# Fused attention and two expert layers: unsplit fp32 scores for two more head pairs, small additions on ScalarE, GpSimd differences in pieces

## The chip, the cores and the metric

The kernel runs on one core of a Trainium2 chip. The metric is the device time of one execution in microseconds (us). The engines are called by the names of the profile: PE (TensorE), DVE (VectorE), ACT (ScalarE), POOL (GpSimd) and SP (SyncE, which issues most of the DMAs). PEld is the load of weights into PE.

## What is computed

Thresholded attention over 4 batches, 8 heads, 576 positions and 64 dimensions per head, then a dense layer with a nonlinearity, then a layer of 8 experts of which each token takes one. All inputs and outputs are fp32.

```python
scores = q @ k.T / sqrt(64)                      # per batch and head
thresh = scores.max(-1) - tau
scores = where(scores >= thresh, scores, -1e9)
attn = exp(scores - scores.max(-1))
attn = attn / (attn.sum(-1) + 1e-9)
x = attn @ v                                     # tokens 2304, width 512
h = x @ w_in                                     # 512 -> 2048
x = (h - tanh(h)) @ w_out                        # 2048 -> 512
# per token: the expert e of the largest of x @ w_gate
y = gate * sigmoid((x @ w_output_gate)[e]) * (relu(x @ w1[e]) @ w2[e])
```

## The kernel before

The work is one long list of operations, written down by a planner in the file itself (class `Sched`): each call `sc.add(engine, duration, due, fn, reads, writes)` adds one operation, and the order in which the operations are emitted on each engine comes from a packed table of numbers, `URGENCY`, one number for each operation. Every engine then works through its own list in that order; an operation whose inputs are not there holds up all behind it on its engine.

Attention goes by units: batch, half of the positions, head pair (4 x 2 x 4 = 32 units, `units`). Batches are counted from 0 in the code, so the second batch is `b == 1`. A unit of the first half has 4 score tiles, one of the second half 5 (the fifth, called merged, holds the last 64 positions of both heads), 144 tiles in all. For each tile (function `attention`):

- PE computes the scores into the PSUM tile `sp`. In the first batch (`full`, the constant `FULL`) this is done in plain fp32, with 64 of the array's rows for one half of the columns and 64 for the other (line 1096). In the others, q and k have been split into two parts of fewer bits, so that four faster matmuls give the same (line 1085).
- DVE reads `sp` from PSUM, writes the negated scaled scores `em` and their minimum `mx` (line 1106). ACT takes the exponential, `e` (line 1109). A threshold `tb = mx + tau` is made on DVE for the two heads of a tile pair at once (line 1118). DVE masks `e` by it and sums (line 1122).
- PE transposes (line 1138), ACT copies the result to `eth`, PE multiplies with V (`pv`, line 1193, in two bursts of 3 and 2 key blocks), and the result is scaled by the reciprocals: on DVE an addition of 1e-9 to the sums `rs` of the unit (line 1160), a reciprocal (line 1162), on ACT and POOL the spread matrices `rb`; the product with them is `xf` (line 1212).

The split of q and k is made by ACT (rounded part, `round_to`) and POOL (difference, `rest`), in `prep_q` and `prep_k`. `rest` cuts POOL's difference into two halves where it has more than `HALVE` = 400 columns. The same helper makes POOL's differences for the dense layer's weights (`wi`, `wo`, from `conv`, whose five steps for a block run on ACT and DVE), for its activations (`gl`) and for the attention's output (`xl`). All DVE and POOL instructions of this kind read and write SBUF; line 1106 reads PSUM.

The dense layer (function `step`, lines 743 and 777, tiles `ph` and `x`) is interleaved with the attention as soon as the first 256 tokens are complete, and fills PE's time between the attention's matmuls. Its weights are stored and fetched again. The expert layer follows after all tokens (lines 1637, 1750, 1783). Buffers are rings: `em` has 5, `e` 3 (`EN`), `rb` 3 (`RBN`).

Of the kernel before, what the change touches and what calls it, by code (L numbers as in the profile page):

```python
# [17 lines left out]
ALU = mybir.AluOpType  # L18
# [3 lines left out]
P = 128  # L22
# [6 lines left out]
CH = 256  # L29
# [20 lines left out]
HALVE = 400  # L50
FULL = 8
EARLY = 4
EMN, EN, ETN, RBN = 5, 3, 2, 3
# [28 lines left out]
    'c-rk)_e0I^`+n_p_Bm}WqbRdfA{k{gsFV_gG^vo35s{EmR%GN|WF{+ARyJj&ge0<8Ml!NWzW4L$^Iv>De#m*9bDrlO*L_{rb24W{Y~J<E^zPq+'  # L82
    '8H0`2J<ACSua*BeJtTN*M&IV|;fvEYmpGpG+ZFq6U4%dD7VBweWWrVdSa2~~mzrN`=UzQII^M2R1@Y-vX*fNp$#=(@@Mz}2y{huJ9Q|~uO>c9%'
    '+hxvAjz>4G^j=Ch&F);+ZMk9bTccMaVssXDy}#@IwLJ<y{nC)w;;JI)I1_xLPM6@C#doi4J>zFEYv<kdm1Z%WUfeWpmSheH(chdEW%)L&xWG5L'
    'aBpidJ=hKp?5s`;vY7w-N8ql9GqsBk4VYP^iCJ*<q21U%^Hy{Y-sC*wlB?dgMTx$KEi0}rk5rUnQ++mmKC>g%XJ@V%u@Ad^ys)#@%hSY?5aN-w'
    'jeb?e?ebgB>b<=riQWDVi5jqaoaq*qSy`d8H@q3@UezsJ?`n#txm874QOTQ~kE&MvB+K|ihEIFZ-v>V!QR<r~_kLUU?PS&CXKY!6{p?Z83H>2g'
    'k{g$q&j~s8ZnFC7@$z!((}^pO+YO)9G{LtZB;mo8HBYb1xKbN<xZf&y{$t0`;x<1s8|-#jxsThH<)4^ZrFQ1{O+%Y&`UeL%>37K1RCqk^IIo9E'
    't$){hkC*3|o=8+MIWmvr$%-|1J688Muz2d>KHVnxSc0la?*#q9Y&G8Me=_n|Xv(&=Khl&FhXfuNGoa-*6Gd!OccunMyKPF}-0%7eZ~K--p$D`r'
    '^Uep<$sYM$IOTunkZp6!@w6WN*B!Q(p3m0G5kl(y3YHGv;PiN5*zCT+JL>`h2iIM#KAVy^dETIP)w1PP>w^vqsb8(Hs`^=+f5Fu8?(YRQWo6p8'
    '7w-7oafa2>ng12M%CG2TX07_F7&zVB>g8S4%NTXRCc`P6PE4Ek^H={9(@VaXnyzT*dM)9)bI$TbQ;Q1&_f*vSzbYf=pQt}PARuAJ0ea#~yY2HW'  # L90
    '>bFNEoHH-o>bJ6M>dWIUznW@3F3`O0Ww}N6GiSh%Wt;XFYHDw#H+FdO+V4ul=BSmf7UA};y<8gl1s?X^RI<56NBT)`>`U4GCSg|Mp~M1>*N!c!'
    'Qhr-#B7QbRGU=Ah!T96}zm<L2micdOHa}hbcjKZt_yzB#_kj^n|7D-{p3$@WSK@1ZxP_C?rDZucmF4@*^?wQ3^^z<n*Xp<<YU8L2t%GA7PsBz|'
    '5?bbr^M4YXPfyZhGX7Bmlhz#es<4Rea<P8$%T33WdJ$TadtHcJdAt)LX&p#k@6h*RpBFltHk^BL^=IYrVe5=PY&p2{o3mA$$?Ec*POtkjSvl*a'
# [318 lines left out]
def pool_tt(n):  # L412
    return int(2.11 * n + (145 if n > 400 else 110 if n < 256 else 60))
# [1564 lines left out]
```

## Time and profile before

| | |
|---|---|
| time, median of 3 runs | 970.16 us (969.92 to 971.55) |
| the profiled execution | 971.04 us |
| its span on the core | 969.2 us |
| PE busy | 940.4 us (97%), 6636 matmuls |
| DVE busy | 727.5 us (75%) |
| ACT busy | 551.1 us (57%) |
| POOL busy | 346.0 us (36%) |

The profiled execution took 971.04 us from end to end, of which 969.2 us are the span from the first to the last instruction. Busy time is the union of an engine's instructions. A PE that is busy is not always at its peak, since matmuls overlap. PE's clock was granted in full through nearly the whole span (1.00 in every stage up to 953 us). Where an engine was idle, the profile names what ended the wait. The score tiles of the first batch run from 4.6 to 83.5 us, and the last score tile at 454.7 us.

### The profile page before, as it was taken

The numbers are of one execution on the slowest core, as the hardware profiler recorded it, in microseconds if no ns is written. First come the engines' busy times: TensorE is split into PE (matmuls) and PEld (weight loads), VectorE is DVE, ScalarE is ACT, GpSimd is POOL, SyncE is SP. The second block draws the span as 40 slices with busy tenths as digits, with TensorE's granted clock in tenths as the row PEclk, the third lists the DMA queues.
The fourth block names the chain that finished last, engine by engine and source line by source line (L and its number), as shares of the span: only waits on it lengthen the run. The fifth ranks groups of instructions, "written<-read, shape, count | busy, mean of one in ns | idle before, by whom it ended". The sixth has DMA issues, their size and how long they took to land.

```text
span 969.2 us, 18499 instructions
## 1 busy us (share of the span) xinstructions
PE 940.4 (97%) x6636; PEld 806.5 (83%) x6636; DVE 727.5 (75%) x1812; ACT 551.1 (57%) x1142; POOL 346.0 (36%) x434
## 2 busy tenths in 40 slices
PE   8899889999999999999999999999999999999996
PEld 4556667888888888888899888888888899999996
DVE  7999999898789877857268668888676777646630
ACT  5888777777778767757445444344343434435421
POOL 1368548884667754434210101011012302213101
PEclk9999999999999999999999999999999999999999
DMA  9264645565664662451595366476854876655600
GB/s 268 102 204 150 195 139 183 170 206 169 198 215 160 193 244 86 132 182 45 180 364 175 118 189 158 130 169 137 266 177 144 271 229 229 193 169 165 214 14 32
DMA packets 71604, 168.70 MB, mean 174 GB/s; under 512 B 32382, under 2 KB 33022, under 8 KB 65616
## 3 DMA queue, kind: packets, MB, share of 16 engines
q1 hardware_dynamic: 67872, 157.41, 51.3%
q0 software_dynamic: 3200, 9.77, 2.9%
q8 instruction: 54, 0.88, 0.4%
q14 instruction: 46, 0.38, 0.1%
q10 hardware_dynamic: 432, 0.26, 0.1%
HBM read 125.99 MB, written 35.45 MB: 167 GB/s over the span
## 4 chain that ended last, share of the span: by engine, by line
PE 81%; DVE 14%; issue 2%; ACT 1%; DMA 1%; POOL 0%; POOLq 0%; DVEq 0%; ACTq 0%
PE x L777 20%; PE ph L743 20%; PE ph L1750 9%; PE py L1637 8%; PE sp L1085 5%; PE pv L1193 5%; DVE em L1122 5%; PE pt L1138 4%; DVE em L1106 3%; PE py L1783 2%; DVE ct L691 1%; PE pt L1682 1%; PE ph L1388 1%; DVE ct L694 1%; DVE tb L1118 1%
## 5 line engine op out<-in xcount | busy, mean ns | idle before, releaser
L743 PE MATMUL ph<-xh,wi 128*128 128x256 f32 x1152 | 178.1, 286 | 1.2 <-DVE u L766 1.1
L777 PE MATMUL x<-wo,gh 128*128 128x512 f32 x576 | 167.7, 404 | 0.0
L743 PEld LDWEIGHTS ph<-xh,wi 128*128 128x128 f32 x1152 | 156.3, 188 | 10.4 <-DVE u L766 3.1
L1122 DVE SCALAR_TENSOR_TENSOR em<-em,tb,e 128x576 f32<-128x576 f32 x144 | 142.4, 1003 | 8.0 <-ACT e L1109 5.0
L1109 ACT ACTIVATE e<-em,mx 128x576 f32<-128x576 f32 x144 | 110.8, 774 | 46.1 <-DVE em L1106 43.3
L1106 DVE TENSOR_SCALAR_CACHE_REDUCE em<-sp 128x576 f32<-128x576 f32 x144 | 107.6, 749 | 36.9 <-PE sp L1085 31.0
L556 POOL TENSOR_SCALAR gh<-u 128x512 fp32r<-128x512 f32 x52 | 38.4, 739 | 220.2 <-DVE u L766 168.5
L777 PEld LDWEIGHTS x<-wo,gh 128*128 128x128 f32 x576 | 99.0, 189 | 16.4 <-issue 1.3
L756 ACT ACTIVATE u<-ph 128x512 f32<-128x512 f32 x72 | 43.0, 598 | 94.2 <-PE ph L743 89.9
L764 DVE SCALAR_TENSOR_TENSOR w<-w,u 128x512 f32<-128x512 f32 x72 | 53.9, 748 | 53.6 <-ACT w L760 53.3
L743 PE MATMUL ph<-xl,wi 128*128 128x256 f32 x576 | 93.5, 284 | 0.0
L1138 PE MATMUL pt<-ident,em 128*128 128x128 f32 x576 | 84.3, 276 | 7.6 <-DVE em L1122 5.2
L554 ACT ACTIVATE eth<-pt 128x512 f32<-128x512 f32 (+1 forms) x160 | 84.6, 548 | 12.5 <-PE pt L1138 11.7
L777 PE MATMUL x<-wo,gl 128*128 128x512 f32 x288 | 90.6, 401 | 0.0
L1138 PEld LDWEIGHTS pt<-ident,em 128*128 128x128 f32 x576 | 65.6, 141 | 22.9 <-ACT eth L554 6.5
L743 PEld LDWEIGHTS ph<-xl,wi 128*128 128x128 f32 x576 | 79.6, 189 | 1.0
L1085 PE MATMUL sp<-kst,qh 128*128 128x288 f32 (+2 forms) x252 | 73.7, 311 | 2.9 <-DVE em L1106 2.8
L1193 PE MATMUL pv<-eth,vt 128*64 128x256 f32 (+1 forms) x512 | 71.6, 414 | 0.9 <-ACT elh L554 0.9
L1619 POOL DMA_INDIRECT out_dram<-o,ids x23 | 24.4, 1059 | 130.9 <-ACT o L1615 127.6
L1755 ACT ACTIVATE hh<-ph 128x320 fp32r<-128x320 f32 (+2 forms) x56 | 22.7, 420 | 83.2 <-PE ph L1750 82.9
L574 DVE TENSOR_TENSOR w<-wraw,w 128x512 fp32r<-128x512 f32 x98 | 65.5, 688 | 5.7 <-ACT w L554 4.3
L1085 PE MATMUL sp<-kst,ql 128*128 128x288 f32 (+2 forms) x252 | 68.0, 293 | 0.0
(380 smaller groups left out, 2003.7 us busy)
## 6 DMA issues: line engine op xcount, KB each, us to landing
wraw<-in_w_dram SPq DMA_DIRECT2D x60, 512.0 KB, 4.5
wi<-wsv SPq DMA_DIRECT2D x17, 1024.0 KB, 5.8
wo<-wsv SPq DMA_DIRECT2D x17, 1024.0 KB, 6.2
craw<-in_w_in_dram SPq DMA_DIRECT2D x14, 512.0 KB, 5.1
craw<-in_w_out_dram SPq DMA_DIRECT2D x14, 512.0 KB, 3.8
kr<-in_kT_dram SPq DMA_DIRECT2D x24, 288.0 KB, 4.6
wsv<-wi SPq DMA_DIRECT2D x6, 1024.0 KB, 4.6
wsv<-wo SPq DMA_DIRECT2D x6, 1024.0 KB, 5.9
```

Source lines behind the costliest of these rows:

```text
L554: return sc.add("ACT", act(n, psum), due, lambda: nc.scalar.activation(dst(), src(), AF.Copy), r, w)
L574: return sc.add(eng, dve(n, psum) + 5 if eng == "DVE" else pool_tt(n), due, lambda: e.tensor_tensor(out=dst(), in0=src(), in1=hi().bitcast ...
L743: nc.tensor.matmul(ph.t[:, j, :], wi.t[:, w_, cc * CH + j * P:cc * CH + (j + 1) * P], x_.t[:, cc, :], start=(n == 0 and cc == 0), stop=(n ...
L777: nc.tensor.matmul(x2b[c, half][t].t, g_.t[:, j, t * P:(t + 1) * P], wo.t[:, w_, j * DM:(j + 1) * DM], start=(first and n == 0 and j == 0) ...
L1085: nc.tensor.matmul(sp.t[:, kb_, o:o + w], q_.t[:, q0:q0 + P], kb.t[:, hh, c0:c0 + w], start=(i == 0), stop=(i == len(todo) - 1),)
L1106: sc.add("DVE", 665, d, lambda ev=ev, sp=sp, mx=mx: nc.vector.tensor_scalar(out=ev().rearrange("p (a b) -> p a b", a=2), in0=sp.t[:, :, 0: ...
L1109: sc.add("ACT", 667, d + 800, lambda e=e, ev=ev, mx=mx: nc.scalar.activation(e.t, ev(), AF.Exp, bias=mx(), scale=-1.0), [(em, h), (m2, h)] ...
L1122: sc.add("DVE", 729, d + TAU, lambda ev=ev, tb=tb, e=e, col=col: nc.vector.scalar_tensor_tensor(out=ev(), in0=ev(), scalar=tb(), in1=e.t, ...
L1138: nc.tensor.matmul(pt.t[:, kt, :], em.t[:, c0:c0 + P], ident, is_transpose=True, start=(kt == 0), stop=(kt == 3))
L1193: nc.tensor.matmul(pvf()[h * D:(h + 1) * D], vb_.t[:, k, :], eth[h].t[:, kt, 0:n] if kt < 4 else elh.t[:, 0:n], start=(kt == 0), stop=(kt ...
L1637: nc.tensor.matmul(py[k].t[:, 0:cap], wx()[:, k * P:(k + 1) * P], x_.t[:, 0:cap], start=(f == 0 and n == 0), stop=(f == 7 and n == 2))
L1750: nc.tensor.matmul(ph.t[:, 0:cap], wx()[:, cc * P:(cc + 1) * P], x_.t[:, cc, 0:cap], start=(n == 0 and cc == 0), stop=(n == 2 and cc == 3))
```

## The change

The diff does six things.

- `FULL` (a count of units, 8) becomes `FULLK` (a count of head pairs, 6): head pairs 0 and 1 of the second batch, which are four units, also get plain fp32 scores from unsplit q and k. Their loads change (`raw_k`, `raw_q` in place of `prep_k`, `prep_q`), and the roundings and differences for them go.
- POOL's differences in `rest` are cut into pieces of at most 144 columns (`FINE`) where they are due before 150 us, and of at most 288 after that.
- The thresholds (80 instructions) and the additions of epsilon (32) go from DVE to ACT.
- In the last two batches the products with V of two units of the first half are made in one run (new function `products`, called when both units' transposes are planned).
- `EN` goes from 3 to 2, `RBN` from 3 to 5.
- The planner's durations for some operations change, and `URGENCY` is a new table, so every engine's list is in a new order.

```diff
-HALVE = 400
-FULL = 8
+HALVE = 288
+FINE = 144
+FINE_T = 150e3
+FULLK = 6
 EARLY = 4
-EMN, EN, ETN, RBN = 5, 3, 2, 3
+EMN, EN, ETN, RBN = 5, 2, 2, 5
+PAIRED = 2
...
-    "x_h": "AP", "x_l": "P", "w_h": "AD", "w_l": "D", "w_l0": "D", "f_h": "A", "thr": "D", "eps": "D", "r_2": "DA",
-    "r_3": "PD", "clamp": "D", "bot": "A", "sum": "D",
+    "x_h": "AP", "x_l": "P", "w_h": "AD", "w_l": "D", "w_l0": "D", "f_h": "A", "thr": "A", "eps": "A", "r_2": "DA",
+    "r_3": "PD", "clamp": "D", "bot": "A", "sum": "D", "xm": "D",
...
     def rest(cls, n, due, dst, src, hi, r, w, psum=False):
         eng = pick(cls) if cls in ENGINES else cls
-        if eng == "POOL" and n > HALVE:
+        if eng == "POOL":
+            np_ = -(-n // (FINE if due < FINE_T else HALVE))
+
             def part(k):
                 a, b, h_ = dst(), src(), hi().bitcast(F32)
                 m = a.shape[1]
-                cut = slice(0, (m + 1) // 2) if k == 0 else slice((m + 1) // 2, m)
+                cut = slice(m * k // np_, m * (k + 1) // np_)
                 nc.gpsimd.tensor_tensor(out=a[:, cut], in0=b[:, cut], in1=h_[:, cut], op=ALU.subtract)
...
-        full = ui < FULL
+        full = 4 * b + hp < FULLK
...
+        waiting.append((ui, dl + TAU, eth, elh, rbs))
+        if half or b < PAIRED or hp % 2:
+            products(waiting)
+            del waiting[:]
+        return dl + 5 * TAU
+
+    waiting = []
+
+    def products(todo):
...
+            for g in BURST if len(todo) == 1 else ():
+                sc.add("PE", (538 if half else 432) * g, dl, lambda k0_=k0_, g=g, pairs_=pairs_: pairs_(range(k0_, k0_ + g)),
+                       [vb_] + [elh] * (k0_ + g == 5) + eth, [(pv, i)], mode=1)
+                k0_ += g
+            runs.append((pairs_, [vb_, elh] + eth))
+            if len(todo) > 1 and i:
+                sc.add("PE", 432 * 10, dl, lambda: [f(range(5)) for f, _ in runs],
+                       [x for _, r in runs for x in r], [(pv, 0), (pv, 1)], mode=1)
...
-        if ui + 1 < FULL:
+        if ui + 1 < len(units) and 4 * units[ui + 1][0] + units[ui + 1][2] < FULLK:
             qnext = raw_q(ui + 1, T0 + 0.5 * TAU)
...
-                (raw_k if 8 * b < FULL else prep_k)(b, 3, T0 + 1 * TAU)
+                (raw_k if 4 * b + 3 < FULLK else prep_k)(b, 3, T0 + 1 * TAU)
```

The new table puts the same kinds of work in other places. Lines move: 1106 becomes 1122, 1118 becomes 1131 (on ACT), 1122 becomes 1138, 1160 becomes 1173 (on ACT), 1162 becomes 1178, 568 becomes 584.

DVE in the first batch, its first half. `em,mx<-sp` is the read of a score tile, `em,rs<-em,tb,e` the mask and sum, `tb` the threshold, `rs<-rs` the epsilon or the reciprocal, `ct` a step of the weights' conversion. Before:

```order
L1122 SCALAR_TENSOR_TENSOR em,rs<-em,tb,e 128x576 x2
L1106 TENSOR_SCALAR em,mx<-sp 128x576
L1160 TENSOR_SCALAR rs<-rs 128x4
L1122 SCALAR_TENSOR_TENSOR em,rs<-em,tb,e 128x576
L1118 TENSOR_SCALAR tb<-mx,tau_t 128x2
L1106 TENSOR_SCALAR em,mx<-sp 128x576
L1122 SCALAR_TENSOR_TENSOR em,rs<-em,tb,e 128x576
L1212 TENSOR_TENSOR xf<-xf,pv 128x256
L1162 RECIPROCAL rs<-rs 128x4
```

DVE at the same place now:

```order
L701 TENSOR_SCALAR ct<-ct 128x512
L1178 RECIPROCAL rs<-rs 128x4
L704 TENSOR_SCALAR ct<-ct 128x512
L1122 TENSOR_SCALAR em,mx<-sp 128x576
L707 SCALAR_TENSOR_TENSOR ct<-craw,ct 128x512
L1138 SCALAR_TENSOR_TENSOR em,rs<-em,tb,e 128x576
L710 SCALAR_TENSOR_TENSOR ct<-craw,ct 128x512
L1138 SCALAR_TENSOR_TENSOR em,rs<-em,tb,e 128x576 x2
L1122 TENSOR_SCALAR em,mx<-sp 128x576
L1256 TENSOR_TENSOR xf<-xf,pv 128x256
```

The thresholds and the epsilon addition are no longer between the reads and the masks; the reciprocal, which stays, now waits for ACT.

ACT at that place; `e` is the exponential, `eth`, `elh` and `xf` are copies from PSUM, `rb` a spread of reciprocals, `kst` the rounded part of a split k. Before:

```order
L1109 ACTIVATE e<-em,mx 128x576 x2
L554 ACTIVATE xf<-pv 128x256
L1109 ACTIVATE e<-em,mx 128x576
L554 ACTIVATE eth_597<-pt 128x4x128
L554 ACTIVATE kst<-kr 128x576 x2
L554 ACTIVATE eth_626<-pt 128x4x128
```

ACT now:

```order
L1131 ACTIVATE tb<-mx,tau_t 128x2 x2
L1125 ACTIVATE e<-em,mx 128x576 x2
L1131 ACTIVATE tb<-mx,tau_t 128x2
L568 ACTIVATE xf<-pv 128x256
L1125 ACTIVATE e<-em,mx 128x576
L568 ACTIVATE eth_609<-pt 128x4x128
L697 ACTIVATE ct<-craw 128x512
L1173 ACTIVATE rs<-rs,eps_t 128x4
L568 ACTIVATE eth_621<-pt 128x4x128
L1125 ACTIVATE e<-em,mx 128x576 x2
```

Thresholds and epsilon stand among the exponentials and the copies that PE waits for, and the rounding of the second batch's k is gone here.

POOL over the second half of the first batch; `kst` and `ql` are differences for k and q, `wi`, `wo` for the dense layer's weights, `xl` for the attention's output, `em` a copy of 64 columns that the merged tile needs. Before:

```order
L568 TENSOR_TENSOR wi_402<-ct,wi_402 128x256 x2
L568 TENSOR_TENSOR kst<-kr,kst 64x288 x4
L574 TENSOR_TENSOR xl<-xf,xh 128x256
L1130 TENSOR_SCALAR em<-em 128x64
L568 TENSOR_TENSOR wo_781<-ct,wo_781 128x256 x2
L1168 TENSOR_SCALAR rb<-blk,rs 128x128
L556 TENSOR_SCALAR xh<-xf 128x256
L574 TENSOR_TENSOR xl<-xf,xh 128x256
L568 TENSOR_TENSOR ql<-qr,qh 128x256 x2
L568 TENSOR_TENSOR kst<-kr,kst 64x288 x4
```

POOL now:

```order
L584 TENSOR_TENSOR wi_420<-ct,wi_420 128x128 x4
L584 TENSOR_TENSOR xl<-xf,xh 128x128 x2
L584 TENSOR_TENSOR wo_746<-ct,wo_746 128x128 x3
L1146 TENSOR_SCALAR em<-em 128x64
L584 TENSOR_TENSOR wo_746<-ct,wo_746 128x128
L570 TENSOR_SCALAR xh<-xf 128x256
L584 TENSOR_TENSOR xl<-xf,xh 128x128
L1184 TENSOR_SCALAR rb<-blk,rs 128x128
L584 TENSOR_TENSOR xl<-xf,xh 128x128
```

The eight k differences and the first q differences are gone, and what is left is in pieces of 128 columns, between which other POOL work now stands.

## Rows read from the trace of the kernel before

**Rows 1.** Busy time by stage; columns: length, then each engine (x instructions), clock, DMA
```profile
0.00:25.00 25.00, 20.83 (x111) 10.39 (x113) 18.80 (x65) 14.21 (x25) 3.13 (x14) 1.00 0.90 265
25.00:150.00 125.00, 110.52 (x781) 75.26 (x778) 122.56 (x302) 102.75 (x212) 75.61 (x94) 1.00 0.49 153
150.00:230.00 80.00, 78.68 (x546) 66.71 (x546) 73.32 (x148) 60.15 (x122) 61.10 (x74) 1.00 0.59 190
230.00:953.00 723.00, 721.67 (x5155) 646.87 (x5154) 511.98 (x1298) 371.81 (x783) 203.86 (x251) 1.00 0.55 176
```

**Rows 2.** Waits of PE's weight loads, 0 to 230 us: total, times, longest
```profile
PEld sp L1096 <- DVE em L1106: 10.7, 21, 1.5
...
PEld sp L1085 <- DVE em L1106: 6.5, 13, 1.0
```

**Rows 3.** DVE by line, 25 to 150 us: busy, mean ns of one | idle before
```profile
L1122 DVE SCALAR_TENSOR_TENSOR em<-em,tb,e 128x576 f32<-128x576 f32 x49 | 49.5, 1016 | 0.6
...
L1118 DVE TENSOR_SCALAR tb<-mx,tau_t 128x2 f32<-128x2 f32 (+1 forms) x27 | 8.5, 318 | 0.2
...
L1160 DVE TENSOR_SCALAR rs<-rs 128x4 f32<-128x4 f32 (+1 forms) x11 | 3.0, 276 | 0.1
```

**Rows 4.** Whole run, single lines: count, duration min/median/max in ns
```profile
L1122 DVE SCALAR_TENSOR_TENSOR em<-em,tb,e x144: 785/851/1565, 8.4 to 457.4; 128x576 f32<-128x576 f32 x144
...
L1106 DVE TENSOR_SCALAR_CACHE_REDUCE em<-sp x144: 708/748/760, 6.0 to 455.8; 128x576 f32<-128x576 f32 x144
...
L1118 DVE TENSOR_SCALAR tb<-mx,tau_t x80: 178/228/910, 8.1 to 456.6; 128x2 f32<-128x2 f32 x64, 128x1 f32<-128x1 f32 x16
...
L1160 DVE TENSOR_SCALAR rs<-rs x32: 156/188/777, 14.8 to 458.3; 128x4 f32<-128x4 f32 x16, 128x5 f32<-128x5 f32 x16
...
L906 ACT ACTIVATE eo<-og x9: 188/203/205, 582.4 to 728.1; 128x2 f32<-128x2 f32 x9
```

**Rows 5.** Timeline of DVE: start, length; a threshold and the step behind it
```profile
27.52 0.22 DVE L1118 TENSOR_SCALAR tb<-mx,tau_t 128x2 f32<-128x2 f32 x1
27.65 0.81 DVE L1122 SCALAR_TENSOR_TENSOR em<-em,tb,e 128x576 f32<-128x576 f32 x1
```

**Rows 6.** POOL by line, 0 to 150 us
```profile
L568 POOL TENSOR_TENSOR kst<-kr,kst 64x288 fp32r<-64x288 f32 x17 | 18.2, 1096 | 6.4 <-ACT kst L554 4.6 <-issue 1.4
L568 POOL TENSOR_TENSOR ql<-qr,qh 128x256 fp32r<-128x256 f32 (+1 forms) x14 | 14.9, 1077 | 9.8 <-ACT qh L554 7.6 <-PE sp L1096 2.2
...
L568 POOL TENSOR_TENSOR wi<-ct,wi 128x256 fp32r<-128x256 f32 x12 | 10.7, 909 | 20.9 <-ACT wi L554 20.8
```

**Rows 7.** POOL's subtractions, shortest durations: 256 columns, then 64 to 256
```profile
L568 POOL TENSOR_TENSOR wi<-ct,wi x24: 725/739/1317, 20.0 to 289.5; 128x256 fp32r<-128x256 f32 x24
...
L574 POOL TENSOR_TENSOR xl<-xf,xh x36: 316/604/1186, 28.3 to 295.1; 128x128 fp32r<-128x128 f32 x12, 128x256 fp32r<-128x256 f32 x8, 128x64 fp32r<-128x64 f32 x8, 128x192 fp32r<-128x192 f32 x8
```

**Rows 8.** ACT by line and shape, 25 to 150 us
```profile
L1109 ACT ACTIVATE e<-em,mx 128x576 f32<-128x576 f32 x48 | 36.7, 774 | 12.8 <-DVE em L1106 12.0 <-DVE rs L1160 0.5
```

**Rows 9.** Timeline of PE: unsplit, split and merged score tiles
```profile
80.65 0.76 PE L1096 MATMUL sp<-kst,ql 64*128 64x288 f32 x4 [1.21 <-DVE em L1106]
81.33 1.84 PE L1193 MATMUL pv<-eth,vt 128*64 128x320 f32 x12
83.15 0.71 PE L1096 MATMUL sp<-kst,ql 64*64 64x288 f32 x8
83.79 0.76 PE L1193 MATMUL pv<-eth,vt 128*64 128x320 f32 x4
...
86.38 0.40 PE L1085 MATMUL sp<-kst,qh 128*128 128x288 f32 x1 [0.70 <-DVE em L1106]
...
87.01 0.60 PE L1138 MATMUL pt<-ident,em 128*128 128x128 f32 x4
...
302.52 0.40 PE L1085 MATMUL sp<-kst,qh 128*128 128x288 f32 x1
...
303.79 0.72 PE L743 MATMUL ph<-xh,wi 128*128 128x256 f32 x4
```

More of the change, by code (lines that the diff above doesn't have):

```diff
@@ L1227, in attention, with pairs_ @@
[L1227 removed]
+        waiting.append((ui, dl + TAU, eth, elh, rbs))
[5 more added lines that the diff above has]
+    def products(todo):
+        dl = todo[-1][1]
+        pv = buf("ps_v", "pv", 1, [P, 4, P])
+        xfs, runs = [], []
+        for i, (ui, _, eth, elh, rbs) in enumerate(todo):
+            b, half, hp = units[ui]
+            n = 320 if half else 256
+            vb_ = vts[b, hp]
+            pvf = lambda i=i, n=n: pv.t.rearrange("p a b -> p (a b)")[:, 256 * i:256 * i + n]
+            def pairs_(kts, pvf=pvf, vb_=vb_, eth=eth, elh=elh, n=n):
+                for kt in kts:
+                    for h in range(2):
+                        nc.tensor.matmul(
+                            pvf()[h * D:(h + 1) * D], vb_.t[:, 2 * kt + h, :],
+                            eth[h].t[:, kt, 0:n] if kt < 4 else elh.t[:, 0:n], start=(kt == 0), stop=(kt == 4))
+            k0_ = 0
+            for g in BURST if len(todo) == 1 else ():
[6 more added lines that the diff above has]
+                       [x for _, r in runs for x in r], [(pv, 0), (pv, 1)], mode=1)
+        for i, (ui, _, eth, elh, rbs) in enumerate(todo):
+            b, half, hp = units[ui]
+            n = 320 if half else 256
+            pvf = lambda i=i, n=n: pv.t.rearrange("p a b -> p (a b)")[:, 256 * i:256 * i + n]
+            xf = buf("ep", "xf", 2, [P, 320])
+            xfs.append(xf)
+            round_to("bot", n, dl + 1200, lambda xf=xf, n=n: xf.t[:, 0:n], pvf, [(pv, i)], [xf], True)
+        for (ui, _, eth, elh, rbs), xf in zip(todo, xfs):
+            b, half, hp = units[ui]
+            n = 320 if half else 256
+            d = dl + 2 * TAU
+            rp = buf("ps_v", "pv", 1, [P, 4, P])
+            rpf = lambda rp=rp: rp.t.rearrange("p a b -> p (a b)")
+            for qt, rb in enumerate(rbs):
+                if qt < 2:
+                    sc.add("PE", 109, d, lambda qt=qt, rb=rb, rp=rp: nc.tensor.transpose(rp.t[:, qt, :], rb.t, ident), [rb], [(rp, qt)])
+                else:
+                    sc.add("PE", 120, d, lambda qt=qt, rb=rb, rp=rp: nc.tensor.matmul(
+                        rp.t[:, qt, 0:D], rb.t, sel, start=True, stop=True), [rb], [(rp, qt)])
+            eng = pick("xm")
+            e_ = nc.vector if eng == "DVE" else nc.gpsimd
+            sc.add(eng, dve(n, True) + 5 if eng == "DVE" else pool_tt(n) + 60, d + 400, lambda rpf=rpf, xf=xf, n=n, e_=e_: e_.tensor_tensor(
+                out=xf.t[:, 0:n], in0=xf.t[:, 0:n], in1=rpf()[:, 0:n], op=ALU.mult), [rp], [xf])
+            t0 = b * S + half * 256
+            o = 0
+            while o < n:
+                c, r = divmod(t0 + o, CH)
+                m = min(CH - r, n - o)
+                xh, xl = chunk(c)
+                hi = lambda xh=xh, r=r, m=m, hp=hp: xh.t[:, hp, r:r + m]
+                src = lambda o=o, m=m, xf=xf: xf.t[:, o:o + m]
+                reg = (hp, r)
+                round_to("x_h", m, d + 1500, hi, src, [xf], [(xh, reg)])
+                rest("x_l", m, d + 1500, lambda xl=xl, r=r, m=m, hp=hp: xl.t[:, hp, r:r + m], src, hi,
+                     [xf, (xh, reg)], [(xl, reg)])
+                o += m
```

304 lines of the change are left out of this document (136 added, 168 removed).

## Prediction

> **What bounds the kernel now.** I read the busy time by stage first [rows 1]. From 230 us to 953 us PE is busy 721.7 of 723 us: it is full, and an idle gap that ends there is worth at most 1.3 us. From 25 to 150 us the picture is another one: DVE is busy 122.6 of 125 us and PE 110.5. PE's 14.5 us of idle time there, 4.2 us before 25 us and 1.3 us between 150 and 230 us are all that waiting costs ahead of the end. What ends the waits is the second view [rows 2]: in the first 230 us PE's loads for the scores waited 10.7 us in 21 cases and 6.5 us in 13 cases on DVE's read of an earlier score tile. So DVE sets the pace up to 150 us, PE after that, and whatever shortens the first stretch moves the rest forward one for one, as long as PE's own work stays the same. The sum of the gain can't be larger than PE's idle time, about 20 us, and some of that is the start.
>
> In that DVE-bound stretch the third view, DVE by line [rows 3], shows where its time goes: 49 masks at 1016 ns, 27 thresholds at 318 ns on two numbers per partition, 11 epsilon additions at 276 ns. The same instructions at their shortest take 785, 178 and 156 ns [rows 4]. The read of a score tile from PSUM takes 708 to 760 ns, whatever runs beside it, while the mask, from and to SBUF, goes from 785 up to 1565 ns. POOL is busy 75.6 us in this stretch, and the stretched instructions are those that read SBUF: DVE waits for POOL there. [...]
>
> **Thresholds and epsilon to ACT.** An instruction's duration runs into the next: a threshold of 0.22 us starts at 27.52 and the mask behind it at 27.65 us [rows 5], so 0.09 us of each duration is overlap. At the durations of the stretch, 27 x (318 - 90) and 11 x (276 - 90) ns give 8.2 us that DVE loses. At the shortest durations, 27 x (178 - 90) and 11 x (156 - 90) ns give 3.1 us: the excess is waiting for POOL, and that may pass to the instruction behind. I take half of the excess as gone: 5.6 us, bounds 3.1 and 8.2. ACT gets the 38 instructions; its nearest row is an activation of two columns, 203 ns [rows 4], so 7.7 us at most, against ACT's 102.8 of 125 us [rows 1]. It loses some rounding for the second batch's q and k, so its load stays near 105 us, below DVE's.
>
> The move adds waits. The epsilon addition on ACT waits for the last mask of a unit, and behind it in ACT's list stand exponentials and copies that PE waits for; the reciprocal on DVE waits for ACT, and masks and reads stand behind it. Nothing in the trace shows this crossing. Its bounds are nothing (the order puts one or two conversion steps between) and one exponential of 774 ns [rows 8] for each of 11 units, 8.5 us. With `EN` = 2 an exponential may start only when the mask two tiles earlier has ended. In the new order 13 of the first 60 tiles have only about 1.4 us of DVE work (a read and a mask) between these masks, in the old order 5; an exponential of 0.77 us and two hand-overs fit into that if ACT isn't busy with something else. I take 1.5 us of new waits for both, nearer the low end, because ACT waited 12.0 us for DVE's reads in this stretch [rows 8] and so has been ahead of DVE.
>
> **Less work on POOL, in pieces.** Of POOL's 94 instructions in the stretch, 8 differences of k at 1096 ns and 8 of q at 1077 ns [rows 6] belong to the four units that are now unsplit: 17.4 us less. But pieces cost: the shortest difference of 256 columns took 725 ns and the shortest of the 64 to 256 column ones, taken as 64 columns, 316 ns [rows 7], so 2.1 ns a column and about 0.18 us for each instruction. By the order some 48 more instructions come in (twice as many for the weights, for `gl`, for `xl` of 256 columns and the remaining k and q), 8.6 us. POOL's time falls by 8.8 of 75.6 us, 12%. The masks' excess, 49 x (1016 - 785) = 11.3 us [rows 3, 4], would fall by 1.3 us with it. What shorter pieces do to the wait of one mask no row shows: between 1.3 us worse (48 x 0.18 us more of POOL, at the share 11.3 / 75.6 that reaches DVE) and half of the excess, 5.6 us better. I take 2.0 us in all, near the proportional 1.3. DVE's relief is then 5.6 + 2.0 = 7.6 us, bounds 1.8 and 13.8.
>
> **Unsplit tiles on PE.** A first-batch tile takes from 80.65 to 81.33 us, 0.68, a split one from 86.38 to 87.01, 0.63 [rows 9]: 16 tiles cost 0.8 us more. The merged tile took 0.64 us (83.15 to 83.79) against 1.27 us split (302.52 to 303.79): two of these save 1.3 us. Together -0.5 us. [...] I take 0, bounds -0.5 and +1.3.
>
> **Paired V products, and the new order.** The order has 35 runs of V products for 41 before, and 373 changes between kinds of matmul for 378 in the attention and dense layer: even if each change cost as much as the 0.05 us between the two kinds of tile above, six fewer are 0.3 us, which I leave out. By the 72nd of 144 score tiles PE's list holds 264 matmuls of the dense layer, 290 before: the mix is nearly the same, so the gain must come from waits. After 230 us the new order can hardly gain, 1.3 us at most, and may lose; I take 0, up to +2.
>
> **The sum,** on the profiled execution of 971.04 us (span 969.2): the stretch from 25 to 150 us -7.6 + 1.5 = -6.1. PE's idle time there falls from 14.5 to 8.4 us, so PE is 93% busy and not yet in the way. Before 25 us, where DVE was idle 6.2 us, -0.5; from 150 to 230 us -0.5 of the 1.3. Together -7.1: 963.9 us, and 963.1 from the median of 970.16, which is 0.9 us below the profiled execution.
>
> **Rivals.** [...]
>
> Second, slower: ACT and DVE run in step. With two `e` buffers and epsilon on ACT, DVE waits at each tile for an exponential that could not be started early. The gain of about 8 us over 49 tiles is eaten from 0.16 us of waiting a tile on; at half of an exponential, 0.39 us, for 24 tiles, plus 0.2 us for 11 reciprocals, DVE loses 11.6 us: 970.2 - 8.1 + 11.6 = 973.7 us. For it: the 13 tight tiles and ACT at 82% of the stretch. Against it: in the run before, masks waited for an exponential in the whole stretch only 0.6 us in all [rows 3].
>
> Third, more: short pieces halve the masks' excess and the thresholds take all of theirs along, 13.8 us of relief, of which PE's 14.5 us of idle can take 12: about 957.5 us.
>
> **Chances.** The forecast, with all between 959 and 968.2 us, 0.56; the larger gain 0.08; no change 0.18; slower 0.18. A difference of 0.2%, about 1.9 us, is the least that a measurement of this kernel can tell from none: faster 0.64, same 0.18, slower 0.18. The range for 8 in 10 goes from the larger gain, 957 us, to just above no change, 972 us; what lies outside is most of the slower case and a little below.
>
> **What would show it.** Right: in the stretch in which DVE is full, DVE's total for 60 tiles falls by 6 to 10 us, masks come down from 1016 towards 950 ns, PE's idle time before 150 us falls by half, and the last score tile comes about 7 us earlier than 454.7 us, with PE as full after 230 us as now. [...] The second shows as waits of masks for `e` or of reciprocals for ACT of more than 5 us in the first 150 us. I would be wrong altogether if PE, full from 230 us on, needed more time there for the same matmuls, or waited there for a weight fetch that comes later in the new order.

## The result, and the profile after

The changed kernel takes 955.52 us in the median (955.15 to 956.71, 4 runs), the kernel before 970.27 us beside it. The ratio is 0.985, with a 95% interval of 0.983 to 0.987: 14.8 us faster, where 7.1 were forecast. The span of the profiled execution is 953.4 us for 969.2.

Busy time by stage of the kernel after (length, then PE, PEld, DVE, ACT, POOL with their instructions, clock, DMA), against [rows 1]:

```profile
0.00:25.00 25.00, 21.90 (x125) 11.50 (x127) 18.93 (x64) 17.31 (x36) 4.92 (x17) 1.00 0.91 275
25.00:150.00 125.00, 119.13 (x851) 78.86 (x850) 114.79 (x283) 110.97 (x256) 87.61 (x145) 1.00 0.51 170
150.00:230.00 80.00, 80.00 (x559) 67.66 (x559) 64.89 (x126) 63.66 (x143) 65.85 (x87) 1.00 0.64 205
230.00:938.00 708.00, 706.13 (x5059) 636.19 (x5056) 484.08 (x1227) 369.30 (x810) 195.22 (x247) 1.00 0.55 174
```

Before 230 us PE is busy 221.0 us, for 210.0 before, and after 230 us it is as full as it was. Its idle time before 150 us falls from 18.7 to 9.0 us, by half, as forecast. From 25 to 150 us DVE is busy 114.8 us for 122.6, though it does more there: 52 masks for 49. POOL is busy 87.6 us for 75.6, where the forecast had it fall by 8.8 us: the pieces cost it more than the unsplit tiles take off.

The waits of PE's weight loads for DVE's reads, 0 to 230 us, against [rows 2] (total, times, longest), have gone from 17.2 to 9.8 us:

```profile
PEld sp L1112 <- DVE em L1122: 7.6, 19, 1.0
...
PEld sp L1101 <- DVE em L1122: 2.2, 3, 1.3
```

DVE by line from 25 to 150 us (busy, mean ns of one, idle before), against [rows 3]:

```profile
L1138 DVE SCALAR_TENSOR_TENSOR em<-em,tb,e 128x576 f32<-128x576 f32 x52 | 46.0, 900 | 3.7 <-ACT tb L1131 3.6
L1122 DVE TENSOR_SCALAR_CACHE_REDUCE em<-sp 128x576 f32<-128x576 f32 x50 | 37.4, 749 | 3.4 <-PE sp L1112 2.0 <-PE sp L1101 1.3
...
L704 DVE TENSOR_SCALAR ct<-ct 128x512 uint32<-128x512 uint32 x12 | 5.6, 468 | 0.1
L701 DVE TENSOR_SCALAR ct<-ct 128x512 f32<-128x512 f32 x12 | 5.5, 459 | 2.0 <-ACT ct L697 2.0
```

Masks take 900 ns for 1016; the read from PSUM takes what it took (749 ns, for 746 in the same stretch before). The new wait of the masks for the threshold on ACT is 3.6 us here. What the moved instructions cost on ACT (min/median/max, whole run), against [rows 4]:

```profile
L1131 ACT ACTIVATE tb<-mx,tau_t x80: 277/293/347, 8.0 to 445.8; 128x2 f32<-128x2 f32 x64, 128x1 f32<-128x1 f32 x16
...
L1173 ACT ACTIVATE rs<-rs,eps_t x32: 282/297/326, 15.8 to 448.0; 128x4 f32<-128x4 f32 x16, 128x5 f32<-128x5 f32 x16
```

The forecast had taken 203 ns as their most.

### The profile page after: what moved, and what is told of

Its sections match the earlier page's. It is cut to its first block, busy times and chain, and to the rows that moved or that the text cites. A ratio compares the mean times of both kernels' runs of the same rounds, so it can differ in the third digit from the quotient of the medians.

```text
span 953.4 us, 18522 instructions
## 1 busy us (share of the span) xinstructions
PE 935.3 (98%) x6632; PEld 801.1 (84%) x6632; DVE 683.5 (72%) x1700; ACT 563.4 (59%) x1246; POOL 355.6 (37%) x496
## 4 chain that ended last, share of the span: by engine, by line
PE 85%; DVE 7%; ACT 3%; issue 3%; POOL 2%; DMA 1%; POOLq 0%; ACTq 0%; SPq 0%; DVEq 0%
PE ph L759 21%; PE x L793 20%; PE ph L1791 9%; PE py L1678 9%; PE pv L1222 6%; PE sp L1101 6%; PE pt L1154 5%; DVE em L1138 2%; PE py L1824 2%; DVE em L1122 2%; PE ph L1429 1%; PE sp L1112 1%; PE pt L1723 1%; PE pt L1692 1%; DMA craw<-in_w_in_dram 1%
## 5 line engine op out<-in xcount | busy, mean ns | idle before, releaser
L1138 DVE SCALAR_TENSOR_TENSOR em<-em,tb,e 128x576 f32<-128x576 f32 x144 | 134.9, 952 | 19.5 <-ACT tb L1131 18.0
L570 POOL TENSOR_SCALAR gh<-u 128x512 fp32r<-128x512 f32 x52 | 35.2, 677 | 228.6 <-DVE u L782 194.7
L793 PEld LDWEIGHTS x<-wo,gh 128*128 128x128 f32 x576 | 98.6, 189 | 14.8 <-issue 0.8
L1101 PE MATMUL sp<-kst,qh 128*128 128x288 f32 (+2 forms) x210 | 61.3, 310 | 1.6 <-DVE em L1122 1.4
L793 PEld LDWEIGHTS x<-wo,gl 128*128 128x128 f32 x288 | 51.1, 188 | 10.6 <-issue 0.9
```

Of the source, the lines that this page charges most:

```text
L793: nc.tensor.matmul(x2b[c, half][t].t, g_.t[:, j, t * P:(t + 1) * P], wo.t[:, w_, j * DM:(j + 1) * DM], start=(first and n == 0 and j == 0) ...
L1101: nc.tensor.matmul(sp.t[:, kb_, o:o + w], q_.t[:, q0:q0 + P], kb.t[:, hh, c0:c0 + w], start=(i == 0), stop=(i == len(todo) - 1),)
L1138: sc.add("DVE", 745, d + TAU, lambda ev=ev, tb=tb, e=e, col=col: nc.vector.scalar_tensor_tensor(out=ev(), in0=ev(), scalar=tb(), in1=e.t, ...
```

## The experiments

### Parts undone or done alone, the order planned anew

In the first eight runs one part was put back or done alone. The planner's numbers of the kernel named were kept for each operation, and the planner laid out a new list from them. 

u1 (in the kernel after) and, the other way round, d1 (in the kernel before) move thresholds and epsilon:

```diff
-    "x_h": "AP", "x_l": "P", "w_h": "AD", "w_l": "D", "w_l0": "D", "f_h": "A", "thr": "A", "eps": "A", "r_2": "DA",
+    "x_h": "AP", "x_l": "P", "w_h": "AD", "w_l": "D", "w_l0": "D", "f_h": "A", "thr": "D", "eps": "D", "r_2": "DA",
```

u2 and, the other way round, d2 change the pieces (`rest` as a whole and `HALVE` are the other kernel's):

```diff
-        if eng == "POOL":
-            np_ = -(-n // (FINE if due < FINE_T else HALVE))
...
+        if eng == "POOL" and n > HALVE:
```

u3, then u4:

```diff
-FULLK = 6
+FULLK = 4
```

```diff
-PAIRED = 2
+PAIRED = 4
```

d3 is the kernel before with the numbers of the kernel after, u5 the kernel after with the numbers of the kernel before, each for the 5546 operations that both have.

> The changed kernel with one part undone: the 80 thresholds and 32 epsilon additions are on DVE again; every other operation is as in the changed kernel, and each operation keeps its number in the order table. The theory now (DVE set the pace up to 150 us, and lost most of what it lost to waits for POOL) expects 5 to 7 us back: 961 to 962.5 us, against 955.5 for the changed kernel. The rival that the new order as such brought the gain expects under 2 us: below 957.5 us. The rival that the unsplit tiles brought it expects the same.

> The changed kernel with POOL's differences cut as before (in two halves above 400 columns, otherwise whole), all else as in the changed kernel. The theory of the waits for POOL expects the masks back from 900 towards 1000 ns in the stretch from 25 to 150 us and 3 to 5 us of time: 958.5 to 960.5 us. The rivals (order, unsplit tiles) expect the masks and the time as in the changed kernel, 955.5 within 1 us.

> The changed kernel with the scores of the second batch's first two head pairs from split q and k again (16 more POOL differences, 8 more ACT roundings, split matmuls). [...] The rival that the unsplit tiles were the main part expects 962 us or more.

> The changed kernel with the V products of each unit on their own, in two bursts, in all batches. PE's busy time fell by 5.1 us with the change, and this run tells whether the pairing did it. The theory (those were small stalls in the DVE-bound stretch) expects 0 to 1 us: 955.5 to 956.5 us. The rival that PE's work itself fell by the pairing expects 958.5 us or more, with PE's busy time up by 3 us or more.

> The kernel before with one part of the change alone: thresholds and epsilon additions on ACT, order numbers as before. The theory that DVE's load in the first 150 us sets the time expects 4 to 6 us less than 970.2: 964 to 966 us. The rival that the order brought the gain expects less than 1.5 us: 968.7 us or more.

> The kernel before with POOL's differences in pieces of at most 144 columns up to 150 us and 288 after, the order numbers as before. The theory of the waits for POOL expects masks of about 950 ns between 25 and 150 us, where they took 1016, and 2 to 4 us less: 966 to 968 us. [...]

> The kernel before with the changed kernel's number for every operation that both have (5546 of 5660), and nothing else of the change. The rival that the order brought the gain expects 962 us or less. The theory of the waits expects 968.5 to 971 us.

> The changed kernel with the numbers of the kernel before for every operation that both have (5546 of 5690), all parts of the change in. The theory of the waits expects most of the gain to stay: 956 to 959 us. The rival that the order brought it expects 965 us or more.

| run | us | ratio to the kernel before, 95% |
|---|---|---|
| u1 | 994.27 | 1.025 (1.024 to 1.027) |
| u2 | 973.25 | 1.003 (1.002 to 1.003) |
| u3 | 980.72 | 1.011 (1.009 to 1.012) |
| u4 | 987.26 | 1.018 (1.017 to 1.020) |
| d1 | 992.09 | 1.022 (1.020 to 1.024) |
| d2 | 987.95 | 1.019 (1.016 to 1.021) |
| d3 | 1005.85 | 1.036 (1.035 to 1.037) |
| u5 | 1002.94 | 1.033 (1.032 to 1.035) |

Every one is slower than the kernel it started from, by 18 to 47 us, undone and done alone alike, and none came where the theory had it (958 to 959.5 us for u3). That can't be the price of the parts: the order was disturbed in each. u4 shows how. Before 230 us its PE is as busy as in the kernel after (221.9 us for 221.0), and it loses behind that, where PE waits some 20 us in all. The longest of PE's waits from 425 to 600 us (total, times, longest), and the stages about it (columns as above):

```profile
PE ph L753 <- DVE u L776: 4.1, 2, 3.9
```

```profile
470.00:485.00 15.00, 15.00 (x105) 13.04 (x104) 4.21 (x16) 4.56 (x10) 4.83 (x9) 1.00 0.39 131
485.00:500.00 15.00, 11.78 (x72) 10.15 (x70) 6.01 (x11) 6.23 (x14) 0.00 (x0) 0.97 1.01 402
500.00:515.00 15.00, 14.13 (x73) 12.64 (x74) 12.63 (x27) 7.24 (x14) 0.70 (x2) 0.80 0.74 279
515.00:530.00 15.00, 15.00 (x96) 13.59 (x97) 12.23 (x22) 7.82 (x16) 1.50 (x2) 1.00 0.47 175
```

PE waits once for 3.9 us, and in the 15 us behind that its granted clock is 0.80 on average, where it is 1.00 ahead of the wait. If the one comes of the other, which one such case doesn't show, the wait is paid twice. So these runs show what a disturbed order costs, and don't price the parts.

### The same parts with the order kept

So the next kernels keep the order: for every operation that stays, its place in the base kernel's list is written into the table, and the planner only follows it (an operation whose inputs come later in that list waits for them).

```diff
+    def listed(self, prio):
+        left = [len(p) for p in self.pred]
+        heap = [(prio[k], k) for k in range(len(left)) if not left[k]]
+        heapq.heapify(heap)
...
+        if not rounds:
+            return self.listed(prio)
```

f1 to f6 combine the edits of u1/d1 and u2/d2 above with this: f1 is u1's edit, f2 u2's, f3 d1's, f4 d2's, f5 both of u1 and u2, f6 both of d1 and d2. On PE, f1, f2 and f5 run exactly the kernel after's list, f3, f4 and f6 that of the kernel before.

> The changed kernel with thresholds and epsilon back on VectorE, every engine keeping the changed kernel's order of work for all else (the earlier runs planned a new order, which cost 18 to 50 us by itself). Theory A, VectorE's load sets the pace until 150 us: the 50 thresholds of that stretch and 11 epsilon steps come back at 178 to 318 and 188 to 276 ns, 11 to 19 us of load, and the masks' waits for ScalarE (some 6 us before 230 us) go: net 5 to 12 us later, 960 to 968 us, and PE's idle time before 230 us grows by that much from 18.1 us. Theory B, the gain is the order's: within 2 us of the changed kernel, 954 to 957.5 us. Theory C, the waits for ScalarE cost more than the load they take off: faster than the changed kernel, 948 to 953 us.

> The changed kernel with GpSimd's differences in the old coarse pieces, all else in the changed kernel's order. Theory A, the length of one GpSimd operation is what VectorE waits for: the masks go back from 900 towards 1016 ns (52 x 0.116 = 6.0 us until 150 us), the conversion steps from 464 towards 560 ns (2.2 us): 4 to 8 us later, 959.5 to 963.5 us. Theory B, GpSimd's total busy time is what counts (it falls by 12 us in that stretch with coarse pieces): no later or even faster, 950 to 956 us. Theory C, the order alone: within 1 us, 954.5 to 956.5 us.

> The kernel before with only the thresholds and the epsilon on ScalarE, in its own order. Theory A (VectorE's load): 8 to 19 us of load go, 6 us of waits for ScalarE come, and the in-order list was laid out for the old cost: 3 to 9 us earlier, 961 to 967 us. Theory B (the order is what gained): 968 to 972 us. Theory C (the hop to ScalarE costs what it saves or more): 970 to 976 us.

> The kernel before with only GpSimd's differences in fine pieces, in its own order. Theory A (length of one GpSimd operation): masks from 1016 towards 900 ns (49 x 0.116 = 5.7 us until 150 us), conversion steps 2.2 us: 4 to 8 us earlier, 962 to 966 us. Theory B (GpSimd's total): 970 to 976 us, since its busy time rises. Theory C (order alone): 969 to 971 us.

> The changed kernel with thresholds and epsilon back on VectorE and coarse GpSimd pieces; what is left of the change is the unsplit tiles, the pairing and the new order. Each alone put back cost 9.1 us (f1) and 6.8 us (f2). Theory A, the two reliefs add up on VectorE: 955.5 + 15.9, 969 to 973 us, so order, pairing and unsplit tiles alone are worth about nothing. Theory B, either missing relief already makes VectorE late and the second costs little more: 964 to 967 us, so order, pairing and unsplit tiles are worth 3 to 6 us by themselves. Theory C, what is left does harm without the reliefs: above 974 us.

> The kernel before with both reliefs (thresholds and epsilon on ScalarE, fine pieces), in its own order. Alone there they gave -0.4 (f3) and +2.4 us (f4). Theory A, the old order holds PE to waits that VectorE's load doesn't set, so the reliefs add up to nothing there either: 970 to 974 us. Theory B, the reliefs need each other (with one alone the wait only moved to the other): 960 to 966 us, and masks near 890 ns with PE's waits for reads and masks both down.

Medians in us, with the ratio to the kernel before and its 95% interval:

| | order of the kernel before | order (and the rest) of the kernel after |
|---|---|---|
| coarse pieces, thresholds and epsilon on DVE | 970.5 (before) | 969.33, 0.999 (0.998 to 1.000) (f5) |
| coarse pieces, on ACT | 970.11, 0.999 (0.998 to 1.000) (f3) | 962.27, 0.991 (0.990 to 0.993) (f2) |
| fine pieces, on DVE | 972.88, 1.002 (1.001 to 1.003) (f4) | 964.62, 0.993 (0.992 to 0.994) (f1) |
| fine pieces, on ACT | 975.63, 1.006 (1.004 to 1.007) (f6) | 955.52, 0.985 (0.983 to 0.987) (after) |

In the right column the two reliefs of DVE are worth 13.8 us together, and all else that the change does is worth 1.2 us without them. In the left column the same two reliefs bring nothing alone and cost 5.1 us together. f1, f2 and f5 came in the range of theory A, f3 and f4 did not (f4 came in that of theory B, POOL's total, which f2 speaks against); f6 ended 1.6 us above its theory A. f3 and f4 by themselves would have spoken for the order as the cause, f5 by itself for the reliefs: neither works without the other. The right column has the unsplit tiles, the pairing and the buffers' new counts too, and no run tells which of these the reliefs need. That it is the order is argued from the waits below, not shown by itself.

What happens in the old order is seen on DVE. The masks from 25 to 150 us in f3, f4 and f6, one row of each:

```profile
L1080 DVE SCALAR_TENSOR_TENSOR em<-em,tb,e 128x576 f32<-128x576 f32 x49 | 48.7, 1000 | 5.9 <-ACT tb L1073 5.5
```

```profile
L1085 DVE SCALAR_TENSOR_TENSOR em<-em,tb,e 128x576 f32<-128x576 f32 x49 | 43.2, 886 | 3.0 <-ACT e L1072 2.3
```

```profile
L1085 DVE SCALAR_TENSOR_TENSOR em<-em,tb,e 128x576 f32<-128x576 f32 x49 | 42.3, 869 | 8.6 <-ACT tb L1078 8.4
```

In f6 masks are the shortest of all, and DVE is busy only 105.8 us. Its waits there (total, times, longest) and the stage:

```profile
DVE em L1085 <- ACT tb L1078: 8.4, 14, 1.4
DVE ct L648 <- ACT ct L644: 5.9, 6, 2.7
DVE rs L1125 <- ACT rs L1120: 3.2, 6, 0.9
```

```profile
25.00:150.00 125.00, 110.92 (x772) 74.29 (x772) 105.84 (x260) 107.33 (x245) 88.46 (x158) 1.00 0.47 152
```

The 16.7 us that DVE no longer works it waits instead, for ACT above all, and PE is busy 110.9 us, for 110.5 in [rows 1]. The list has masks and conversion steps in places where their inputs used to be ready ([rows 3] has 0.6 us of idle time before the masks), and they no longer are. The one wait of 5.7 us in f4 goes further back, to a fetch of weights:

```profile
DVE ct L648 <- ACT ct L644: 8.2, 5, 5.7
```

```profile
ACT ct L644 <- DMA craw<-in_w_in_dram: 5.4, 1, 5.4
```

(the first is DVE's waits, the second ACT's, in f4 from 25 to 150 us). This one wait is the whole of f4's loss: compared matmul by matmul, f4 is 1.8 us ahead of the kernel before at 65 us and 3.9 us behind it at 75 us. The fetch was issued at 63.4 us, for 62.2 in the kernel before, behind a load of q in SyncE's list that waited 4.4 us, for 2.0, until POOL's pieces of `ql` were done. In the kernel after the masks wait 3.6 us for ACT's thresholds there and the conversion steps 2.0.

What the pieces do to a mask goes the same way in either order. The same row in f1 (fine), f2 and f5 (coarse), and f2's stage:

```profile
L1086 DVE SCALAR_TENSOR_TENSOR em<-em,tb,e 128x576 f32<-128x576 f32 x50 | 43.2, 875 | 1.8 <-ACT e L1073 0.7 <-DVE tb L1082 0.5
```

```profile
L1084 DVE SCALAR_TENSOR_TENSOR em<-em,tb,e 128x576 f32<-128x576 f32 x50 | 47.8, 969 | 3.3 <-ACT tb L1077 3.2
```

```profile
L1084 DVE SCALAR_TENSOR_TENSOR em<-em,tb,e 128x576 f32<-128x576 f32 x47 | 43.4, 934 | 1.1 <-ACT e L1071 0.3
```

```profile
25.00:150.00 125.00, 116.46 (x816) 75.86 (x812) 115.47 (x273) 108.26 (x246) 67.67 (x85) 0.99 0.49 162
```

With coarse pieces masks take 934 to 1016 ns in the four kernels, with fine ones 869 to 900, although POOL is busy 20 us longer (87.6 us in 145 instructions in the kernel after, for 67.7 in 85 in f2). So the time of a mask goes with the length of POOL's operations, not with POOL's total. In the new order masks also got longer when the thresholds left DVE: from 875 to 900 ns with fine pieces (f1 to after), from 934 to 969 with coarse ones (f5 to f2).

f1, f2, f5 and the kernel after run the same 6632 matmuls in the same order, so their traces can be laid side by side, matmul by matmul. How many us each is behind the kernel after, at the matmul that the kernel after starts at the time given, and at the end of the span:

| | 25 us | 150 us | 230 us | 400 us | 800 us | end |
|---|---|---|---|---|---|---|
| f1 | 1.4 | 4.8 | 5.4 | 7.8 | 7.9 | 9.6 |
| f2 | -0.6 | 4.7 | 5.1 | 5.5 | 5.5 | 7.0 |
| f5 | 1.4 | 9.7 | 11.2 | 14.2 | 14.2 | 14.1 |

Of the 14 us between f5 and the kernel after, 11.2 are won by 230 us and 3.0 from there to 400 us, while attention still runs. f1 and f2 lose their last 1.6 us in one place in the expert layer, near 858 us, where PE waits 1.5 us for DVE; f5 and the kernel after have no such wait. Why f1 and f2 have it stays open.

The page's line for PE in f5 and after:

```profile
PE 942.1 (97%) x6632; PEld 802.1 (83%) x6632; DVE 719.8 (74%) x1812; ACT 546.6 (56%) x1134; POOL 329.7 (34%) x418
```

```profile
PE 935.3 (98%) x6632; PEld 801.1 (84%) x6632; DVE 683.5 (72%) x1700; ACT 563.4 (59%) x1246; POOL 355.6 (37%) x496
```

PE's idle time falls by 7.3 us (967.5 - 942.1 = 25.4 to 953.4 - 935.3 = 18.1), its busy time for the same list by 6.8. So PE's busy time fell for the same list. Whether short waits that it held made this was not shown; before 150 us a transpose took 273 ns in the median in both, at most 421 in f5 and 331 in the kernel after. All of the fall lies in the first 400 us; behind that the two agree within 0.1 us. The transposes of the whole run have 1.4 us of it (f5, then after: busy, mean ns, idle before):

```profile
L1100 PE MATMUL pt<-ident,em 128*128 128x128 f32 x576 | 84.4, 277 | 4.7 <-DVE em L1084 3.3 <-DVE sel L455 0.5 <-ACT eth L516 0.5
```

```profile
L1154 PE MATMUL pt<-ident,em 128*128 128x128 f32 x576 | 83.0, 275 | 2.0 <-DVE em L1138 1.3 <-DVE sel L507 0.5
```

### Unsplit tiles and pairing, the order kept

f7 is u3's edit and f8 u4's, in the kernel after's order. Both need a few operations moved, since pieces of work exist in one kernel and not in the other.

> The changed kernel with batch 2's first two head pairs split as in the kernel before, in the changed kernel's order (pieces that it has not stand where the kernel before has them, and some steps had to move behind what they read). Theory A (VectorE's load makes the gain): the unsplit tiles are worth little on PE (-0.5 to +1.3 us), but the split ones take 8 more GpSimd/ScalarE steps: 955 to 959 us. Theory B (the unsplit tiles earn much of the gain, by what they take off ScalarE and GpSimd): 961 us or more.

> The changed kernel with the V products in the old, unpaired succession, else in the changed kernel's order. Theory A: pairing moves no work on any engine, 954.5 to 957 us. Theory B (pairing frees the transposed tiles earlier and takes waits off ScalarE's copies): 958 us or more, with longer PE waits for ScalarE's copies before 230 us.

f7 took 1006.42 us, ratio 1.038 (1.036 to 1.040), f8 977.53 us, 1.008 (1.006 to 1.009). By their times both would count for theory B, but neither is a price. In f7 PE is busy 96.3 of 125 us from 25 to 150 us: the steps that had to move hold up the score tiles behind them (PE waited 14.7 us for DVE's reads before 230 us). f8's stages:

```profile
25.00:150.00 125.00, 120.06 (x858) 80.33 (x855) 115.23 (x283) 112.01 (x258) 89.66 (x146) 1.00 0.52 173
150.00:230.00 80.00, 79.69 (x556) 66.67 (x554) 64.38 (x125) 62.44 (x141) 63.88 (x83) 1.00 0.59 198
230.00:450.00 220.00, 206.31 (x1446) 173.89 (x1447) 142.79 (x319) 152.26 (x346) 107.62 (x151) 0.98 0.45 151
```

Until 230 us it is at the pace of the kernel after, as u4 was; the loss begins behind that. So the pairing is no source of the gain before 230 us, where most of the gain was made. What it is worth behind that, and what the unsplit tiles are worth, stays open. f5 gives only their sum with the new order and the buffers' new counts, without the reliefs: 1.2 us.

### VectorE's load by itself, and the epsilon

f9 leaves the kernel after as it is and adds DVE's old threshold ahead of the masks, written to a place that nothing reads. f10 puts back the epsilon alone (`"eps": "D"`), in the kernel after's order.

```diff
+                    if first:
+                        nc.vector.tensor_scalar(
+                            out=spare[:, 0:nt], in0=m2.t[:, 0:nt], scalar1=tau_t, scalar2=None, op0=ALU.add)
                     return nc.vector.scalar_tensor_tensor(
```

> The changed kernel, thresholds and epsilon on ScalarE as they are, and the old VectorE threshold instruction added before the masks that follow it: it reads the same minima and writes a place that nothing reads, so it is load on VectorE and nothing else; order unchanged. Theory A, VectorE's load until 150 us is the price: 32 thresholds there took 8.9 us in f1, of which some fill waits for ScalarE (about 4 us): 959.5 to 964.5 us, masks' and reads' waits on PE growing. Theory B, it was not the load but where the result is made that counted: 955 to 957 us.

> The changed kernel with only the epsilon step back on VectorE, all else in its order. In f1 the epsilon steps until 150 us took 3.0 us of VectorE; in the changed kernel the reciprocals waited 4.4 us for ScalarE, in four places over the whole run. Theory A (load counts): 1 to 3 us later, 956.5 to 958.5 us. Theory B (the wait for ScalarE costs more than the load): 952 to 955 us, which would beat both kernels.

f9 took 960.93 us, ratio 0.990 (0.988 to 0.992), 5.4 us more than the kernel after, and f10 957.44 us, 0.987 (0.985 to 0.988), 1.9 us more, about what can be told from nothing. Both came in the range of theory A. The added instructions in f9, 0 to 150 us:

```profile
L1141 DVE TENSOR_SCALAR spare<-mx,tau_t 128x2 f32<-128x2 f32 (+1 forms) x32 | 9.6, 301 | 0.0
```

The 48 others, behind 150 us, took 17.7 us more. So 27.3 us of load cost 5.4 us of time: DVE's load is paid for by itself, wherever the threshold is made, and it is paid for mostly where DVE is full. The profiled execution of f9 (962.08 us, the slowest of four) is 4.2 us behind the kernel after by 150 us. If the two parts of f1's 9.1 us add, the epsilon is 1.9 and the thresholds 7.2, of which f9's load gives 5.4. In f1 the two took 11.9 us on DVE before 150 us.

## Why the prediction fell short

The direction, and the place of most of the gain, were right: most of it was made before 230 us, DVE's reads hold up PE less, masks came down and PE is as full behind as it was. The last score tile comes 10.9 us before the 454.7 us of the kernel before, where 7 were forecast:

```profile
L1101 PEld LDWEIGHTS sp<-kst,ql x210: 187/188/192, 101.4 to 443.8; 128*128 128x128 f32 x105
```

The size was half of what came. By stage the sum had 0.5 us before 25 us, 6.1 from 25 to 150 us, 0.5 up to 230 us and nothing behind that. The two reliefs by themselves brought 1.4, 8.3, 1.5 and 3.0 us (f5's row). Five steps to name.

- **Pieces.** The step "I take 2.0 us in all, near the proportional 1.3" was the most mis-sized. From 25 to 150 us the pieces brought 5.3 us (f2's row), and 4.9 with the thresholds on DVE (f5's less f1's); over the whole run 6.8 and 4.7. The step took POOL's total busy time as the measure, and had that fall by 8.8 us. It rose by 12.0: f5, with the unsplit tiles and the rest of the change, has 64.1 us for 75.6, 11.5 less; f2 has 3.5 more than f5; and f2's 85 instructions in the stretch became 145 for 19.9 us more, 0.33 us for each and not 0.18. Masks got shorter all the same, by 59 and 69 ns in the new order and by 130 in the old one, and the conversion steps, which the sum left out, went from 555 and 568 to 468 and 459 ns, some 2.3 us for 24 of them. The upper bound, half of the excess or 5.6 us, was the better value.
- **Thresholds and epsilon.** The step "I take half of the excess as gone: 5.6 us", less 1.5 us for new waits, gave 4.1 us. In the stretch it was about right: 3.4 us with fine pieces (f1's row), 3.0 with coarse ones (f5's less f2's). Part of the excess did pass to the masks, 25 and 35 ns for each, 1.3 and 1.8 us over some 50, and the masks' waits for ACT were 3.6 us, with 293 ns for an instruction on ACT and not 203. What the step missed lies outside of the stretch: 1.4 and 2.0 us before 25 us, and 3.0 and 3.7 from 150 to 400 us. Over the whole run the move is worth 9.1 and 7.1 us. The wait of 1.5 us in the expert layer, which f1 and f2 alone have, is in the 9.1, and in the 6.8 of the pieces; the 7.1 and the 4.7 are less by it.
- **The ceiling.** The steps "an idle gap that ends there is worth at most 1.3 us", of the time behind 230 us, and "The sum of the gain can't be larger than PE's idle time" took busy time as untouchable. The total stayed under their 20 us, but of the 14.1 us between the spans of f5 and after, 6.8 came out of PE's busy time, and 3.0 were won behind 230 us. Nothing in the sum allowed for that.
- **The new order.** It was put at 0 and added to the rest. By itself it is worth little, as said (1.2 us with all that goes with it), but the terms don't add: with the rest as it was before, the two reliefs together cost 5.1 us, with the rest of the change they bring 13.8. The sum left out this condition.
- **Unsplit tiles on PE** were put at 0, with an upper bound of 1.3 us that no run shows. In the kernel after, an unsplit tile among the dense layer's matmuls takes 0.68 us (84.74 to 85.42 and 93.33 to 94.01 us), the 0.68 of the first batch [rows 9]. What they are worth in the whole run stays open.

Of the rivals the third, more, came nearest, with 957.5 us, and it had been given too little weight. The number is partly luck. It had 12 us in the stretch from 25 to 150 us, where the reliefs brought 8.3, and next to nothing beside it. Masks lost 116 ns of their excess of 231, the half that it named, but the thresholds did not take all of their excess along. No change had a chance of 0.18. That the wait only moves holds in part: those 1.3 and 1.8 us have moved to the masks, and with the rest as it was before the wait moves altogether (f3: 970.11 us, f6 with 16.7 us of DVE's work turned into waits), though to ACT, and not to the masks' durations. The second, ACT and DVE in step, shows as 6.2 us of the masks' waits for thresholds before 230 us in 11 cases; the reciprocals waited 4.4 us in the whole run.

## What to carry to other kernels

In a kernel whose engines follow lists laid out by hand or by a planner, a relief of one engine may be worth nothing without the plan that goes with it, and the plan little without its relief: here +5.1 us and -1.2 us apart, -14.8 us together. To price a part, keep the list of everything else as it is, and read a difference in a re-planned kernel as the price of the new plan. Where an engine's instructions grow longer beside another's, as DVE's masks did beside POOL's differences, try shorter operations on the one that isn't the bound, even if its total grows (here 969 to 900 ns a mask for 20 us more of POOL); and don't take the idle time of a full engine as the most that can be gained, since its busy time can fall for the same list (here from 942.1 to 935.3 us).

## What the runs showed of the hardware

- A threshold takes 293 ns in the median on ACT (277 to 347), for 228 on DVE [rows 4], 64 of two columns and 16 of one in either; the activation of two columns that the forecast leaned on took 203 ns [rows 4]. That one is an exponential without a bias, `tb` and `rs` are an identity with a bias from a tile; which of these makes the 90 ns no run shows.
- POOL's differences cut in two raised its busy time by 20 us in the stretch from 25 to 150 us (67.7 in f2 to 87.6 in the kernel after) and lowered the mask's mean on DVE from 969 to 900 ns.
- After a wait of 3.9 us on a PE that had been full (u4), the granted clock was 0.80 on average over the next 15 us, and 1.00 again behind that.
- The same matmuls in the same order took 942.1 us of PE's busy time in f5 and 935.3 in the kernel after, at a mean granted clock of 0.996 and 0.997.
